# A chunked attention stage whose products are cut by heads, with the bonus term as a product on TensorE

## The chip, the cores and the metric

One core of a Trainium2 chip runs one program with one launch. The metric is device time in microseconds (us) from the program's start to its end. The engines are TensorE (PE; its weight loads are shown apart as PEld), VectorE (DVE), ScalarE (ACT), GpSimd (POOL) and SyncE (SP), on which all transfers are issued. Each works through its instructions in the order in which they were written, and waits for the others by semaphores.

## The reference

```python
def _attn_ref(r, k, v, w, u):                    # B=4, H=8, S=768, D=48
    state = np.zeros((B, H, D, D))
    for t in range(S):
        kt, vt, rt = k[:, :, t], v[:, :, t], r[:, :, t]
        cur = np.einsum('bhd,bhe->bhde', u[None] * kt, vt)
        y[:, :, t] = np.einsum('bhd,bhde->bhe', rt, state + cur)
        state = w[None, :, :, None] * state + np.einsum('bhd,bhe->bhde', kt, vt)
...
x = _moe_ref(attn_out as 3072 tokens x 384)      # x @ w_in, mish, @ w_out
return _moe2_ref(x)                              # 8 experts, weights from a Sinkhorn-scaled gate
```

The state is one 48x48 matrix for each batch row and head. It decays by `w` at each step. The bonus term is `cur`: at its own step a token's `v` counts with the weight sum over d of r·u·k.

## The kernel before

All is float32. The attention is done in chunks of 128 steps: a unit `i` is a chunk `c` (0 to 5) of a batch row `b` (0 to 3), `i = 4c + b`, so 24 units. Two heads form a pair: their 48 rows stand at partitions 0 to 47 and 64 to 111 of a tile of 112, and four pairs `p` stand side by side. In each unit

- `ld` holds r and k with the head's dimension on partitions (112 x 2 x 4 x 128); `lt` holds k and r with time on partitions, `lv` holds v so;
- `rt` and `kd` (DVE) are r and k times powers of the decay; `sc` (PE, `a_scores`) are the products of a head's kd and rt, 48 rows each, two heads on the two halves of the array's rows;
- `A` (128 x 128 for each head) gets the bonus weights `bc` on its diagonal by eight ACT instructions (`a_diag`), and the scores above the diagonal by two predicated copies on DVE (`a_tri`); `bc` is made by two POOL products (`a_q`) and a DVE reduction (`a_b`);
- `ya` (`a_out`) sums, for each pair, the state times rt and, for the two heads, `vz` times A. `vz` is v spread by ACT (`a_vz`) to 96 columns of which one head's half is zero, so that both heads add into the same 96 rows;
- `un` (`a_kv`) is the chunk's own state, kh (k times decay, DVE) times v, for whole pairs; ACT masks the blocks that mix two heads (`a_mask`), and four DVE instructions add it to the decayed state `st` (`a_state`);
- ACT copies `ya` to `xT`, the next layer's input (`a_evac`): one instruction for three pairs and three of 32 rows for the fourth.

A table `steps` of functions and unit offsets is walked once for each `i`; it alone sets the order on every engine. Beside this, every second iteration converts one weight tile of the next layer (`a_cv`: four DVE instructions on `v` and `q`, an ACT copy `wm`; then a subtraction and an addition on POOL). The banks of PSUM are named by tags: the scores take three banks in turn, `un` takes `y0` and `y1` in turn, `ya` has `y2` alone. After the last unit the first expert layer begins (`first`, line 246), from `xs`, the input split into two parts by ACT and POOL (`split_x`).

Of the kernel before, what the change touches and what calls it, by code (L numbers as in the profile page):

```python
# [21 lines left out]
NP = H // 2  # L22
# [25 lines left out]
NVZ = 3  # L48
# [32 lines left out]
def layers(ctx: ExitStack, tc: tile.TileContext, a, out, bad, general):  # L81
# [388 lines left out]

    def chunked_attention(aw, ac):
        KD0 = 1
        EQ1, EQ2, EKD, EKH, ECS, ECA, EXS = pool, pool, dve, dve, pool, pool, pool
        aunits = [(c, b) for c in range(NC) for b in range(B)]
        NA = len(aunits)
        ld, lt, lv = {}, {}, {}

        def load_d(i):
# [3 lines left out]
            lt[i] = aw.tile([128, 2, DM], F32, name=f"lt{i}", tag="lt", bufs=3)  # L482
            nc.sync.dma_start(lt[i], a["kr"][b, c])

        def load_v(i):
            c, b = aunits[i]
            lv[i] = aw.tile([128, DM], F32, name=f"lv{i}", tag="lv")
            nc.sync.dma_start(lv[i], a["v"][b, c])
# [28 lines left out]
        vzs = []  # L517
        for i in range(NVZ):
            vz = wA.tile([128, NP, 2, DD], F32, name=f"vz{i}", tag="w")
            pool.memset(vz, 0.0)  # L520
            vzs.append(vz)

# [25 lines left out]
        def tables():  # L548
            powers(64, 192)
            Wh = me.tile([DR, NP, C], F32, name="Wh", tag="p", bufs=MB[2])  # L550
            dve.tensor_copy(Wh, Wp[:, :, 63:191][:, :, ::-1])
            for p in range(NP):
                tp = bank([128, 128], f"tp{p}", f"y{p % 3}")
                pe.matmul(tp[:, 0:DR], Wh[:, p, :], ident[:DR, :DR], start=True, stop=True)
                act.activation(Wkh[:, p], tp.rearrange("t (j d) -> t j d", j=2)[:, :, 0:D], AF.Copy)
# [8 lines left out]
        st2 = [wA.tile([DR, 2, NP, DD], F32, name=f"st{b}", tag="w") for b in range(B // 2)]  # L564
        st = [st2[b // 2][:, b % 2] for b in range(B)]
        T = [{} for _ in aunits]

        def a_vz(i):
            vz = vzs[i % NVZ]
            vh = lv[i].rearrange("t (p j d) -> t p j d", p=NP, j=2)  # L570
            for j in range(2):
                act.activation(vz[:, :, j, j * D:(j + 1) * D], vh[:, :, j, :], AF.Copy)
            T[i]["vz"] = vz
# [5 lines left out]
        def a_q(i):  # L579

            q = me.tile([128, DM], F32, name=f"aq{i}", tag="y", bufs=MB[3])
            (dve if aunits[i][0] == NC - 1 else EQ1).tensor_tensor(q, lt[i][:, 1], ub, op=ALU.mult)
            EQ2.tensor_tensor(q, q, lt[i][:, 0], op=ALU.mult)
            T[i]["q"] = q

        def a_b(i):
            bc = aw.tile([128, H], F32, name=f"bc{i}", tag="bc")
            dve.tensor_reduce(bc, T[i]["q"].rearrange("t (h d) -> t h d", h=H), axis=AX.X, op=ALU.add)
            T[i]["bc"] = bc
# [31 lines left out]
        def a_kv(i):  # L621
            if aunits[i][0] == NC - 1:
                return
            un = bank([DR, NP, DD], f"un{i}", f"y{i % 2}")
# [5 lines left out]
        def a_mask(i):  # L630
            c, b = aunits[i]
            if c == NC - 1:
                return
            um = st[b] if c == 0 else T[i]["un"]
            for j in range(2):
                act.activation(um[:, :, j * D:(j + 1) * D], T[i]["un"][:, :, j * D:(j + 1) * D], AF.Copy,
                               scale=hm[:, j:j + 1])
            T[i]["um"] = um

        def a_state(i):  # L640
            c, b = aunits[i]
            if 0 < c < NC - 1:
                for p in range(NP):
                    dve.scalar_tensor_tensor(st[b][:, p, :], st[b][:, p, :], w128[:, p:p + 1], T[i]["um"][:, p, :],
                                             op0=ALU.mult, op1=ALU.add)

        def a_out(i):
            c, b = aunits[i]
            x = T[i]
            y = bank([DD, NP, C], f"ya{i}", "y2")  # L650
            for p in range(NP):
                if c > 0:
                    pe.matmul(y[:, p, :], st[b][:, p, :], x["rt"][:, p, :], start=True, stop=False)  # L653
                for j in range(2):
# [12 lines left out]

        def a_cv(i):

            m = (i - 1) // 2  # L670
            if 0 <= m < NCA:
                if i % 2:
                    for _ in conv_bits(m):
                        pass
                    conv_act(m)
                else:
                    conv_sub(m, ECS)
                    conv_add(m, ECA)
# [8 lines left out]
        a_vz(0)  # L687
        for i in range(NA + 1):
            for fn, d in steps:
                if i == NA and fn is a_out:  # L690
                    first(0)
                    first(1)
                if (0 <= i + d < NA or fn is a_cv) and (i + d > 0 or d <= 0) and not (i == 0 and fn in (a_rt, a_kd)):
                    fn(i + d)
                if i == 0 and fn is a_scores:
                    tables()
                    a_b(0)
                    a_rt(1)
                    a_kd(1)
                    a_kh(0)  # L700
                    marks()
            if NA - 4 < i < NA:
                xss.setdefault((-1, 0), []).append(split_x(0, i + 3 - NA, "xs", EXS))
        last.append(lambda: a_evac(NA - 1))

    def stepwise_attention(ac):
# [6 lines left out]
        sel = ac.tile([DR, 3 * D - 1], F32, name="sel")  # L713
        pool.memset(sel, 0.0)
        for j in range(2):
            nc.sync.dma_start(sel[:, (j + 1) * D - 1:(j + 1) * D], a["hmask"][:, j:j + 1])
# [6 lines left out]
        rk = ac.tile([DR, 2, NC, C], F32, name="rk")  # L723
        for b in range(B):
            for p in range(NP):
# [3 lines left out]
                y = [bank([DD, S // 2], f"yg{b}_{p}_{g}", f"y{2 * (p % 2) + g}") for g in range(2)]  # L729
                for e in range(D):  # L730
# [9 lines left out]
                    for g in range(2):  # L740
                        pe.matmul(y[g], sel[:, D - 1 - e:3 * D - 1 - e], x[:, g * S // 2:(g + 1) * S // 2],
                                  start=(e == 0), stop=(e == D - 1))
                for c in range(NC):
# [3 lines left out]
                    if p < KI:  # L747
                        act.activation(xt[0:DD, p, x0:x0 + C], yc, AF.Copy)
                    else:
                        for k in range(KI):  # L750
                            act.activation(xt[DD:128, k, x0:x0 + C], yc[32 * k:32 * k + 32, :], AF.Copy)
# [878 lines left out]
def _lay_out(x):  # L1630
# [17 lines left out]
    tm = [t(z, (B, H, NC, C, D), (0, 2, 3, 1, 4)).reshape(B, NC, C, 1, DM) for z in (k, r)]  # L1648
    a["kr"] = np.ascontiguousarray(np.concatenate(tm, axis=3))
# [4 lines left out]
    a["ub"] = np.ascontiguousarray(np.broadcast_to(u.reshape(1, DM), (128, DM)))  # L1654
# [5 lines left out]
    perm = np.stack([np.where(p < DD, i * DD + p, 3 * DD + 32 * i + p - DD) for i in range(KI)])  # L1660
# [24 lines left out]
```

## Time and profile before

| | |
|---|---|
| median of 3 runs (lowest to highest) | 2024.33 us (2023.33 to 2024.84) |
| the profiled execution's own time | 2026.27 us |
| its span, first to last instruction | 2024.5 us |
| TensorE busy in the span | 1990.4 us, 98% |
| VectorE, ScalarE, GpSimd busy | 67%, 53%, 37% |
| first product of scores | 8.66 us |
| first product of the expert layer | 144.03 us |

The rows are read so: an engine's busy time is the union of its instructions in a stretch; a float32 product is two records (x16 are eight products). "idle before, releaser" is how long the engine had nothing running and what ended that. PEclk is the mean TensorE clock that was granted, 1.00 being 2.4 GHz and 0.50 being 1.2 GHz.

### The profile page before, as it was taken

What the parts mean: (1) busy time and instruction counts of PE and PEld (TensorE: products, weight loads), DVE (VectorE), ACT (ScalarE), POOL (GpSimd) and SP (SyncE); (2) the same over time, 40 slices, a digit from 0 to 9 for tenths busy, and PEclk for the clock granted to TensorE, in tenths of its full rate; (3) what the DMA queues carried; (4) which work ended last, traced back from release to release, by engine and by line L of the source; (5) the groups of instructions that cost most, each with busy time, mean ns of one, the idle gap of its engine ahead of it and who ended that gap; (6) DMA issues with size and microseconds to landing.
All of it is one profiled execution on the core that took longest, in us unless ns stands there. A gap on an engine that the chain in (4) does not pass through costs nothing.

```text
span 2024.5 us, 27279 instructions
## 1 busy us (share of the span) xinstructions
PE 1990.4 (98%) x9334; PEld 1647.8 (81%) x9334; DVE 1360.1 (67%) x2177; ACT 1063.1 (53%) x2204; POOL 751.6 (37%) x639
## 2 busy tenths in 40 slices
PE   8899999999999999999999999999999999999998
PEld 7888888887778888877878888888888888888887
DVE  8998889778787777678764455555465555455554
ACT  7998888888755545444443433343344343333332
POOL 5546565557554333355561243311044011011110
PEclk8999999999999999999999999999999999999999
DMA  8750111010246655655465665558545566445440
GB/s 255 214 150 30 32 32 40 24 35 1 96 154 234 228 207 192 203 211 201 156 225 165 189 215 194 190 153 262 162 151 155 135 182 226 141 151 159 143 120 33
DMA packets 169156, 305.96 MB, mean 151 GB/s; under 512 B 39664, under 2 KB 85424, under 8 KB 169008
## 3 DMA queue, kind: packets, MB, share of 16 engines
q1 hardware_dynamic: 169008, 304.13, 46.7%
q8 instruction: 76, 1.25, 0.3%
q14 instruction: 72, 0.59, 0.1%
HBM read 226.90 MB, written 77.17 MB: 150 GB/s over the span
## 4 chain that ended last, share of the span: by engine, by line
PE 89%; DVE 5%; ACT 2%; issue 2%; POOL 1%; DMA 1%; DVEq 0%; SPq 0%; POOLq 0%; ACTq 0%
PE y L1039 37%; PE Bk L907 16%; PE U L907 15%; PE ph L246 9%; PE x L331 9%; ACT A L606 1%; PE ya L655 1%; DVE tc L939 1%; DVE A L619 1%; PE un L626 0%; DMA lv<-in_v_dram 0%; PE sc L614 0%; ACT xT L666 0%; DVE r L826 0%; PE ya L653 0%
## 5 line engine op out<-in xcount | busy, mean ns | idle before, releaser
L1039 PE MATMUL y<-gf,w 128*128 128x512 f32 x2088 | 570.4, 390 | 0.0
L1039 PEld LDWEIGHTS y<-gf,w 128*128 128x128 f32 x2088 | 391.0, 188 | 82.5 <-DVE gf L1031 1.5
L1039 PE MATMUL y<-ge,w 128*128 128x512 f32 x1368 | 373.8, 390 | 0.0
L1062 POOL TENSOR_TENSOR xT<-xT,xT 128x512 f32<-128x512 f32 x102 | 142.3, 1410 | 577.3 <-DVE xT L1061 576.0
L1029 ACT ACTIVATE gf<-tc 128x512 fp32r<-128x512 f32 x232 | 146.5, 632 | 389.6 <-DVE tc L939 375.6
L939 DVE TENSOR_TENSOR tc<-tc,Bk 128x512 f32<-128x512 f32 x270 | 185.1, 685 | 237.8 <-PE Bk L907 222.3
L939 DVE TENSOR_TENSOR tc<-tc,U 128x512 f32<-128x512 f32 x270 | 185.3, 686 | 222.7 <-PE U L907 208.3
L1039 PEld LDWEIGHTS y<-ge,w 128*128 128x128 f32 x1368 | 256.2, 188 | 53.5 <-DVE ge L1031 0.5
L1029 ACT ACTIVATE ge<-tc 128x512 fp32r<-128x512 f32 x152 | 96.1, 632 | 248.3 <-DVE tc L939 237.6
L331 PE MATMUL x<-g,wm 128*128 128x512 f32 x864 | 212.2, 390 | 0.3 <-POOL g L320 0.2
L246 PE MATMUL ph<-xs,wm 128*128 128x512 f32 x864 | 212.0, 390 | 0.3 <-POOL xs L216 0.3
L1031 DVE SCALAR_TENSOR_TENSOR gf<-tc,gf 128x512 fp32r<-128x512 f32 x232 | 193.5, 837 | 22.9 <-ACT gf L1029 18.2
L246 PEld LDWEIGHTS ph<-xs,wm 128*128 128x128 f32 x864 | 161.8, 188 | 36.5 <-POOL xs L216 0.7
L331 PEld LDWEIGHTS x<-g,wm 128*128 128x128 f32 x864 | 161.8, 188 | 35.2 <-DVE xT L347 0.8
L320 POOL TENSOR_TENSOR g<-y,g 128x512 fp32r<-128x512 f32 x96 | 125.0, 1302 | 102.2 <-ACT g L315 95.6
L937 ACT ACTIVATE tc<-Bk 128x512 f32<-128x512 f32 x192 | 114.3, 595 | 85.3 <-PE Bk L907 78.7
L937 ACT ACTIVATE tc<-U 128x512 f32<-128x512 f32 x192 | 114.4, 596 | 83.5 <-PE U L907 78.7
L907 PE MATMUL Bk<-xc,wc 128*128 128x512 f32 x540 | 152.0, 390 | 0.9 <-DVE tc L939 0.9
L907 PE MATMUL U<-xc,wc 128*128 128x512 f32 x540 | 151.7, 389 | 0.0
L1031 DVE SCALAR_TENSOR_TENSOR ge<-tc,ge 128x512 fp32r<-128x512 f32 x152 | 127.7, 841 | 21.4 <-ACT ge L1029 15.7
L847 POOL TENSOR_TENSOR w<-r,w 128x384 fp32r<-128x384 f32 x64 | 68.6, 1074 | 186.6 <-ACT w L846 175.4
L907 PEld LDWEIGHTS Bk<-xc,wc 128*128 128x128 f32 x540 | 101.1, 188 | 23.0 <-DVE tc L939 1.8
(256 smaller groups left out, 3210.9 us busy)
## 6 DMA issues: line engine op xcount, KB each, us to landing
wc<-keep SPq DMA_DIRECT2D x208, 384.0 KB, 3.7
w<-keep SPq DMA_DIRECT2D x128, 384.0 KB, 5.5
keep<-wc SPq DMA_DIRECT2D x104, 384.0 KB, 3.6
r<-in_w_dram SPq DMA_DIRECT2D x128, 192.0 KB, 3.7
keep<-w SPq DMA_DIRECT2D x64, 384.0 KB, 3.0
ld<-in_rkT_dram SPq DMA_DIRECT2D x24, 448.0 KB, 4.8
pb<-prow SPq DMA_DIRECT2D x42, 256.0 KB, 8.5
lt<-in_kr_dram SPq DMA_DIRECT2D x24, 384.0 KB, 5.1
```

The costliest lines, as they stand in the source:

```text
L246: pe.matmul(ph, w[:, pw, k, :], xs[:, px, :], start=(m == 0), stop=(m == 3 * KI - 1))
L320: pool.tensor_tensor(gs[i][:, 1], y, gs[i][:, 0].bitcast(F32), op=ALU.subtract)
L331: pe.matmul(sums[n][k], wo[f][:, pw, k, :], g[:, px, :], start=(f == f0 and m == 0), stop=(f == f1 and m == 1), skip_group_check=True)
L606: act.activation(A[:, h % 2, h // 2, :], ident, AF.Copy, scale=T[i]["bc"][:, h:h + 1])
L847: eng.tensor_tensor(flat(t[:, 1]), src, flat(t[:, 0]).bitcast(F32), op=ALU.subtract)
L907: pe.matmul(out_, w[:, pw, :], x[px], start=bool(start and m == 0), stop=bool(stop and m == 2), skip_group_check=True)
L937: act.activation(t, b, AF.Copy, scale=1.0 if kind == "c" else -1.0)
L939: dve.tensor_tensor(t, t, b, op=ALU.add if kind == "+" else ALU.subtract)
L1029: act.activation(g[:, 0], t, AF.Relu)
L1031: return lambda: dve.scalar_tensor_tensor(g[:, 1], t, 0.0, g[:, 0].bitcast(F32), op0=ALU.max, op1=ALU.subtract)
L1039: pe.matmul(Y[t][k], w[:, pw, k, :], x[:, px, :], start=(f % NF2 == 0 and m == 0), stop=(f % NF2 == NF2 - 1 and m == 2), skip_group_check= ...
L1062: pool.tensor_tensor(o, o, t_, op=ALU.add)
```

## The change

- `a_out`: the two heads of a pair no longer add into the same 96 rows. Each head's v (64 or 48 columns of `lv`, no `vz`) gives rows 0 to 63 or 64 to 111 of `ya`, on one half of the array's columns (a tile of 128 x 64). All eight of them stand first in a row, then the four products of the state, for whole pairs of 112 rows. The 16 rows between two heads get values that nothing uses.
- The bonus: `a_q` is one POOL product of r and k in `ld`'s layout (112 x 512); `a_bc` sums it with u in four TensorE products of 8 columns (`us` holds u in the right places), into the last 8 columns of the bank of `un`; ACT copies the result to `bc`. So `lt` needs no r and is half as large; the tile `ub` and the DVE reduction go.
- The state `st` is 112 x 112 for a pair, zero off the heads' blocks, and `un` is not masked: `a_decay` multiplies the whole state by the decay on POOL, `a_add` adds the two blocks on DVE (in chunk 0 ACT copies them).
- `kh` goes from DVE to POOL (but for the first unit), the addition of the weight conversion goes one iteration later, and v's tiles have four buffers for two.
- `a_evac` copies 112 rows of three pairs, and the fourth pair to a tile `stg`; when 512 columns of it are there, six transfers put its rows into the gaps of `xT`. The rows of `w_in` are permuted on the host to match.

```diff
-        steps = ((load_d, 3), (a_tri, -1), (a_scores, 0), (a_kv, 0), (a_out, -1), (load_v, 2),
-                 (a_q, 1), (a_state, -2), (a_kh, 1), (a_evac, -2), (a_rt, 1), (a_diag, 0),
-                 (a_cv, 0), (a_mask, -1), (a_vz, 1), (a_kd, 1), (a_b, 1))
+        steps = ((load_d, 3), (a_tri, -1), (a_add, -2), (a_scores, 0), (a_out, -1), (a_kv, 0),
+                 (a_q, 1), (a_bc, 1), (a_kh, 1), (a_evac, -2), (a_b, 0), (a_rt, 1), (a_diag, 0),
+                 (a_cv, 0), (a_kd, 1), (a_decay, -1), (load_v, 2))
...
+            q = me.tile([DR, NP, C], F32, name=f"aq{i}", tag="y", bufs=MB[3])
+            pool.tensor_tensor(q, ld[i][:, 0], ld[i][:, 1], op=ALU.mult)
...
+        def a_bc(i):
+            bp = T[i - 1]["ub"] if i else bank([128, TT], "ub", "y1")
+            T[i]["bp"] = bp[:, TT - H:TT]
+            for p in range(NP):
+                pe.matmul(T[i]["bp"], T[i]["q"][:, p, :], us[:, p, :], start=(p == 0), stop=(p == NP - 1))
...
+        def a_decay(i):
+            c, b = aunits[i]
+            if 0 < c < NC - 1:
+                pool.tensor_tensor(st[b], st[b], w128.unsqueeze(2).to_broadcast([DR, NP, DR]), op=ALU.mult)
...
+                if c == 0:
+                    act.activation(s, n, AF.Copy)
+                else:
+                    dve.tensor_tensor(s, s, n, op=ALU.add)
...
             for p in range(NP):
-                if c > 0:
-                    pe.matmul(y[:, p, :], st[b][:, p, :], x["rt"][:, p, :], start=True, stop=False)
-                for j in range(2):
-                    pe.matmul(y[:, p, :], x["vz"][:, p, j, :], x["A"][:, j, p, :],
-                              start=(c == 0 and j == 0), stop=(j == 1))
+                for j, w in enumerate((64, D)):
+                    pe.matmul(y[64 * j:64 * j + w, p, :], lv[i][:, p * DD + j * D:p * DD + j * D + w], x["A"][:, j, p, :],
+                              start=(p == 0), stop=(c == 0 and p == NP - 1), skip_group_check=True)
+            if c > 0:
+                for p in range(NP):
+                    pe.matmul(y[:, p, :], st[b][:, p, :], x["rt"][:, p, :], start=False, stop=(p == NP - 1),
+                              skip_group_check=True)
...
-            act.activation(xt[0:DD, :, x0:x0 + C], y[:, 0:KI, :], AF.Copy)
-            for k in range(KI):
-                act.activation(xt[DD:128, k, x0:x0 + C], y[32 * k:32 * k + 32, KI, :], AF.Copy)
+            act.activation(xt[0:DR, :, x0:x0 + C], y[:, 0:KI, :], AF.Copy)
+            act.activation(stg[n][0:DR, x0:x0 + C], y[:, KI, :], AF.Copy)
+            if i == ends[n]:
+                spread_heads(n, stg[n])
```

On TensorE, one iteration before, in the middle chunks (`sc` scores, `un` the chunk's state, `ya` the output; two of the four equal pairs of `ya` are shown, the rest alike):

```order
L614 MATMUL sc_145<-rt_770,kd_787 128x128
L626 MATMUL un_805<-lv_681,kh_183 112x96 [waits DMAHW1_49,DVE_49,Activation_49]
L626 MATMUL un_805<-lv_681,kh_183 112x96 x3
L653 MATMUL ya_810<-rt_695,st_187 96x128 [waits PE_49,Activation_49]
L655 MATMUL ya_810<-A_772,vz_153 96x128 x2
L653 MATMUL ya_810<-rt_695,st_187 96x128
L655 MATMUL ya_810<-A_772,vz_153 96x128 x2
```

The same stretch of the changed kernel (the products of 64 and 48 rows alternate four times; the first two are shown), with the bonus products `un<-us,aq` at its end:

```order
L612 MATMUL sc_150<-rt_495,kd_507 128x128
L652 MATMUL ya_527<-A_497,lv_385 64x128 [waits PE_49,Activation_49]
L652 MATMUL ya_527<-A_497,lv_385 48x128 [waits DVE_49]
...
L656 MATMUL ya_527<-rt_428,st_185 112x128 x4
L625 MATMUL un_540<-lv_452,kh_181 112x96 [waits DMAHW3_49,Pool_49]
L625 MATMUL un_540<-lv_452,kh_181 112x96 x3
L582 MATMUL un_540<-us,aq_545 128x8 [waits Pool_49]
L582 MATMUL un_540<-us,aq_545 128x8 x3
```

The output moved ahead of the chunk's state, `un` now waits for POOL, and four products of 8 columns came in behind it.

On GpSimd, two iterations before (`aq` the bonus, `v` and `wm` the weight conversion):

```order
L582 TENSOR_TENSOR aq_683<-lt_513,ub 128x384 [waits DMAHW1_49,DVE_49]
L583 TENSOR_TENSOR aq_683<-aq_683,lt_513 128x384 [waits Pool_49]
L582 TENSOR_TENSOR aq_758<-lt_584,ub 128x384 [waits DMAHW5_49,DVE_49]
L583 TENSOR_TENSOR aq_758<-aq_758,lt_584 128x384 [waits Pool_49]
L171 TENSOR_TENSOR v_706<-v_706,wm_712 128x384 [waits DVE_49,Activation_49]
L176 TENSOR_TENSOR wm_712<-v_706,q_707 128x384 [waits DVE_49,Pool_49]
```

And two iterations of the changed kernel, where `st` is the decay of a state:

```order
L575 TENSOR_TENSOR aq_813<-ld_645 112x512 [waits DMAHW6_49,Pool_49]
L597 TENSOR_TENSOR kh_180<-lt_647,Wkh 128x8x48 [waits DMAHW7_49,PE_49,Pool_49]
L175 TENSOR_TENSOR wm_708<-v_702,q_703 128x384 [waits DVE_49,Pool_49]
L632 TENSOR_TENSOR st_185<-st_185,w_184 112x448 [waits PE_49]
L575 TENSOR_TENSOR aq_885<-ld_717 112x512 [waits DMAHW2_49]
L597 TENSOR_TENSOR kh_181<-lt_719,Wkh 128x8x48 [waits DMAHW3_49,PE_49]
L170 TENSOR_TENSOR v_836<-v_836,wm_842 128x384 [waits DVE_49,Activation_49]
L632 TENSOR_TENSOR st_187<-st_187,w_184 112x448 [waits PE_49]
```

Six instructions in two iterations became eight, one conversion step stands in each iteration, and the decay, last in each, waits for TensorE.

On VectorE, one iteration with a weight conversion in the changed kernel (before, a `kh`, four `st` of 112x96 and a reduction `bc` stood there too, and `st` waited for PE and ACT):

```order
L617 COPY_PREDICATED A_1032<-tri,sc_149 128x512 [waits PE_49,Activation_49]
L644 TENSOR_TENSOR st_191<-st_191,un_942 48x4x48 [waits Pool_49]
L644 TENSOR_TENSOR st_191<-st_191,un_942 48x4x48
L591 TENSOR_TENSOR rt_1092<-ld_913,Wr 112x512 [waits DMAHW4_49]
L141 TENSOR_SCALAR v_1104<-raw_844 128x384 [waits DMAHW7_49]
L143 SCALAR_TENSOR_TENSOR v_1104<-raw_844,v_1104 128x384 [waits DVE_49]
L154 TENSOR_SCALAR q_1105<-v_1104 128x384 [waits DVE_49]
L156 SCALAR_TENSOR_TENSOR q_1105<-raw_844,q_1105 128x384 [waits DVE_49]
L570 TENSOR_TENSOR kd_1114<-ld_913,Wk 112x512
```

The addition to the state now stands ahead of `rt`, the conversion and `kd`, and waits for POOL's decay.

## Rows read from the trace of the kernel before

**Rows 1.** Windows: busy us (and instructions) by engine, PEclk, DMA share, GB/s.
```profile
8.66:40.20 31.54, 27.07 (x192) 24.53 (x192) 27.92 (x50) 22.90 (x76) 18.90 (x19) 0.73 0.93 265
40.20:119.09 78.89, 71.91 (x674) 66.61 (x673) 75.11 (x164) 72.06 (x230) 41.81 (x39) 0.96 0.77 225
119.09:146.17 27.08, 23.60 (x217) 20.98 (x216) 24.62 (x52) 26.48 (x84) 11.89 (x12) 1.00 0.39 121
146.17:2024.50 1878.33, 1862.67 (x8227) 1530.72 (x8227) 1227.35 (x1905) 938.83 (x1810) 674.67 (x553) 1.00 0.45 146
```

**Rows 2.** Lines of VectorE, 40.20 to 119.09: busy us, mean ns, idle before.
```profile
L619 DVE COPY_PREDICATED A<-tri,sc 128x512 f32<-128x512 uint8 x28 | 18.7, 719 | 1.5 <-ACT A L606 1.5
L644 DVE SCALAR_TENSOR_TENSOR st<-st,w,un 112x96 f32<-112x96 f32 x52 | 13.1, 303 | 1.6 <-PE ya L653 1.6
L599 DVE TENSOR_TENSOR kh<-lt,Wkh 128x384 f32<-128x384 f32 x14 | 10.9, 778 | 0.0
L588 DVE TENSOR_REDUCE bc<-aq 128x8 f32<-128x384 f32 x14 | 7.6, 541 | 0.0
...
L157 DVE SCALAR_TENSOR_TENSOR q<-raw,q 128x384 f32<-128x384 uint32 x7 | 3.9, 559 | 0.2
```

**Rows 3.** Lines of ScalarE, 40.20 to 119.09.
```profile
L606 ACT ACTIVATE A<-ident,bc 128x128 f32<-128x128 f32 x112 | 34.3, 388 | 0.4
L666 ACT ACTIVATE xT<-ya 32x128 f32<-32x128 f32 x42 | 11.2, 266 | 0.5
L636 ACT ACTIVATE un<-un,hm 112x192 f32<-112x192 f32 x28 | 11.0, 393 | 0.8
L572 ACT ACTIVATE vz<-lv 128x192 f32<-128x192 f32 x27 | 8.2, 352 | 0.0
```

**Rows 4.** Lines of GpSimd, 40.20 to 119.09.
```profile
L171 POOL TENSOR_TENSOR v<-v,wm 128x384 f32<-128x384 f32 x7 | 7.1, 1009 | 21.2 <-ACT wm L164 15.8 <-DVE q L157 2.9 <-DVE kd L577 2.5
```

**Rows 5.** Timeline of TensorE over one unit: start us, us, instruction.
```profile
85.48 1.16 PE L614 MATMUL sc<-rt,kd 48*128 48x128 f32 x16
86.57 1.02 PE L626 MATMUL un<-lv,kh 128*112 128x96 f32 x8
87.43 0.38 PE L653 MATMUL ya<-rt,st 112*96 112x128 f32 x2
87.65 0.60 PE L655 MATMUL ya<-A,vz 128*96 128x128 f32 x4
...
90.16 1.16 PE L614 MATMUL sc<-rt,kd 48*128 48x128 f32 x16
```

**Rows 6.** Timeline of VectorE and of GpSimd in an iteration with a conversion.
```profile
31.82 1.24 DVE L157 SCALAR_TENSOR_TENSOR q<-raw,q 128x384 f32<-128x384 uint32 x1
32.98 0.67 DVE L577 TENSOR_TENSOR kd<-ld,Wk 112x512 f32<-112x512 f32 x1
...
31.43 1.21 POOL L582 TENSOR_TENSOR aq<-lt,ub 128x384 f32<-128x384 f32 x1 [1.92 <-DVE v L144]
32.72 1.20 POOL L583 TENSOR_TENSOR aq<-aq,lt 128x384 f32<-128x384 f32 x1
```

**Rows 7.** Windows before and after the last of three falls of TensorE's clock.
```profile
100.00:104.00 4.00, 2.60 (x25) 2.04 (x24) 4.00 (x11) 3.88 (x13) 3.46 (x4) 1.00 0.69 185
104.00:108.00 4.00, 4.00 (x24) 4.00 (x24) 3.46 (x8) 2.67 (x9) 1.50 (x2) 0.57 1.00 271
```

**Rows 8.** Timeline of the first units: weight loads of a table's products, the third unit's scores.
```profile
11.20 1.78 PEld L554 LDWEIGHTS tp<-ident,Wh 112*128 112x128 f32 x8 [0.76 <-DVE Wh L551]
23.03 1.16 PE L614 MATMUL sc<-rt,kd 48*128 48x128 f32 x16
```

**Rows 9.** Timeline of the end: the last unit's scores, the split input, the product it releases.
```profile
139.36 1.31 PE L614 MATMUL sc<-rt,kd 48*128 48x128 f32 x16
...
144.83 1.28 POOL L216 TENSOR_TENSOR xs<-xT,xs 128x512 fp32r<-128x512 f32 x1 [3.38 <-ACT xs L215]
...
146.17 1.19 PE L246 MATMUL ph<-xs,wm 128*128 128x512 f32 x4 [0.27 <-POOL xs L216]
```

More of the change, by code (lines that the diff above doesn't have):

```diff
@@ L47 @@
 NWA = 24
-NVZ = 3
 NG = 3
@@ L469, in layers, with spread_heads @@
     last = []
+    def spread_heads(n, src):
+        for k in range(KI):
+            for j in range(2):
+                nc.sync.dma_start(xT[n][64 * j + D:64 * j + 64, k, :], src[64 * j + 16 * k:64 * j + 16 * k + 16])
     def chunked_attention(aw, ac):
         KD0 = 1
-        EQ1, EQ2, EKD, EKH, ECS, ECA, EXS = pool, pool, dve, dve, pool, pool, pool
+        EKD, ECS, ECA, EXS = dve, pool, pool, pool
         aunits = [(c, b) for c in range(NC) for b in range(B)]
@@ L476, in chunked_attention @@
         ld, lt, lv = {}, {}, {}
+        stg = [wA.tile([128, TT], F32, name=f"stg{n}", tag="w") for n in range(NT)]
         def load_d(i):
@@ L562, in marks @@
             dve.scalar_tensor_tensor(okw, wT, W_MAX, okw, op0=ALU.is_le, op1=ALU.mult)
-        st2 = [wA.tile([DR, 2, NP, DD], F32, name=f"st{b}", tag="w") for b in range(B // 2)]
-        st = [st2[b // 2][:, b % 2] for b in range(B)]
+        st = []
+        for b in range(B):
+            st.append(wA.tile([DR, NP, DR], F32, name=f"st{b}", tag="w"))
+            pool.memset(st[b], 0.0)
         T = [{} for _ in aunits]
-        def a_vz(i):
-            vz = vzs[i % NVZ]
-            vh = lv[i].rearrange("t (p j d) -> t p j d", p=NP, j=2)
-            for j in range(2):
-                act.activation(vz[:, :, j, j * D:(j + 1) * D], vh[:, :, j, :], AF.Copy)
-            T[i]["vz"] = vz
+        ends = {(b * NC + c) // NSUB: i for i, (c, b) in enumerate(aunits)}
         def a_kd(i):
@@ L633, in a_mask @@
                 return
-            um = st[b] if c == 0 else T[i]["un"]
             for j in range(2):
[L636 to L645, printed above, removed]
+                r = slice(64 * j, 64 * j + D)
+                s, n = st[b][r, :, r], T[i]["un"][r, :, j * D:(j + 1) * D]
+                if c == 0:
+                    act.activation(s, n, AF.Copy)
+                else:
+                    dve.tensor_tensor(s, s, n, op=ALU.add)
         def a_out(i):
@@ L686, in chunked_attention @@
         a_q(0)
-        a_vz(0)
         for i in range(NA + 1):
@@ L723, in stepwise_attention @@
         rk = ac.tile([DR, 2, NC, C], F32, name="rk")
+        stg = [wA.tile([128, TT], F32, name=f"stg{n}", tag="w") for n in range(NT)]
         for b in range(B):
@@ L728, in stepwise_attention @@
                 rT, kT = (rk[:, j].rearrange("d c t -> d (c t)") for j in range(2))
-                y = [bank([DD, S // 2], f"yg{b}_{p}_{g}", f"y{2 * (p % 2) + g}") for g in range(2)]
+                y = [bank([DR, S // 2], f"yg{b}_{p}_{g}", f"y{2 * (p % 2) + g}") for g in range(2)]
                 for e in range(D):
@@ L747, in stepwise_attention @@
                     if p < KI:
-                        act.activation(xt[0:DD, p, x0:x0 + C], yc, AF.Copy)
+                        act.activation(xt[0:DR, p, x0:x0 + C], yc, AF.Copy)
                     else:
-                        for k in range(KI):
-                            act.activation(xt[DD:128, k, x0:x0 + C], yc[32 * k:32 * k + 32, :], AF.Copy)
+                        act.activation(stg[blk // NSUB][0:DR, x0:x0 + C], yc, AF.Copy)
+        for n in range(NT):
+            spread_heads(n, stg[n])
     if general:
@@ L1653, in _lay_out @@
     a["vT"] = t(v, (B, NP, 2, S, D), (0, 1, 2, 4, 3))
-    a["ub"] = np.ascontiguousarray(np.broadcast_to(u.reshape(1, DM), (128, DM)))
+    a["us"] = np.zeros((DR, NP, H), f4)
+    for h in range(H):
+        a["us"][64 * (h % 2):64 * (h % 2) + D, h // 2, h] = u.reshape(H, D)[h]
     a["ident"] = np.eye(128, dtype=f4)
@@ L1659, in _lay_out @@
     p = np.arange(128)
-    perm = np.stack([np.where(p < DD, i * DD + p, 3 * DD + 32 * i + p - DD) for i in range(KI)])
+    j, d = p // 64, p % 64
+    perm = np.stack([np.where(d < D, i * DD + j * D + d, 3 * DD + j * D + 16 * i + d - D) for i in range(KI)])
     wi = np.asarray(x["moe_w_in"])[perm.reshape(-1)]
```

53 lines of the change are left out of this document (23 added, 30 removed).

## The prediction

> **What bounds the kernel now.** I cut the span at four products of TensorE that stand in both kernels [rows 1]. From 146.17 us on TensorE is busy for 1862.67 of 1878.33 us: the expert layers, which the change doesn't touch. What the attention gains or loses reaches the end unshortened; nothing later can absorb it. Ahead of that lie 146 us in three parts: the start up to the sixth unit (31.54 us), fourteen units of the middle chunks (78.89 us, 5.63 each) and the last units (27.08 us). In the middle part VectorE is busy for 75.11 us, ScalarE for 72.06, TensorE for 71.91, GpSimd for 41.81. The first two share the bound: 5.37 and 5.15 us a unit. TensorE alone would need less: where nothing holds it, a unit takes 90.16 - 85.48 = 4.68 us [rows 5].
>
> **What each engine gives and gets,** for a unit of the middle chunks.
>
> *VectorE* loses the four `st` (4 x 0.303), `kh` (0.778) and the reduction (0.541) [rows 2] and gets two additions of 48 x 192. They read PSUM like `st`, and I price them like it, 0.3 each; below lies nothing, above `kh`. That is 5.37 - 2.53 + 0.6 = 3.4 us.
>
> *ScalarE* loses two `vz` (2 x 0.352), two masks (2 x 0.393) and three copies of 32 rows (3 x 0.266); the copy of the fourth pair is one of these again, and the bonus copy of 8 columns is between nothing and 0.27; I take 0.2. So 5.15 - 2.29 + 0.47 = 3.3 us [rows 3].
>
> *GpSimd* had two products and, in the mean, one conversion step of 1.009 [rows 4]. Now it has q (512 columns, as the split input: 1.28 [rows 9]), `kh` (384 columns: 1.01), a conversion step (1.01) and the decay (448 columns: between, 1.15): 4.45 us instead of 41.81 / 14 = 3.0. No row has a broadcast operand, as the decay has; I keep 1.01 and 1.28, the rows of 384 and of 512 columns, as its bounds.
>
> *TensorE*: scores 1.09 as before (85.48 to 86.57), `un` 0.86 (86.57 to 87.43), the four products of the state 0.22 each as before [rows 5]. The eight products of `vz` cost 0.22 each, 1.76. The eight column products are the unknown. The nearest rows are the scores, where two heads share the array by rows and eight products take 1.09; on the other side they cost 1.76 as before. I take 1.09, because the same number of columns streams through two halves. The four bonus products stream 8 columns but load 128 of weights twice each; eight loads of 112 columns take 0.86 with `un`, and sixteen under the scores 1.09, so 0.55 to 0.9; I take 0.9. Sum 1.09 + 1.09 + 0.88 + 0.86 + 0.9 = 4.82 us.
>
> The Trainium skill, in "TensorE: Matmul & The Clock Gate", Part 3 under "What overlaps and what doesn't", says that a weight load runs beside a product in flight only when the row groups differ. The two column halves use the same rows, so by this rule each load would stand alone. The trace speaks against it: with `un` on all rows, eight loads and eight products together take 0.86 us. By the row the output costs 1.09; by the rule it would be at least the old 1.76, which is the third rival.
>
> **The path that then sets the middle part.** The orders show a loop that was not there. The decay of unit j waits for the last product of `ya` of unit j; the addition waits for the decay and stands ahead of `rt`, the conversion and `kd`; the next scores wait for `kd`. One lap is two iterations, one of them with a conversion. What lengthens it is that VectorE and GpSimd get in each other's way [rows 6]: the conversion's last step took 1.24 us for its mean of 0.56 [rows 2], because GpSimd's product ran until 31.43 + 1.21 = 32.64, and ended 0.42 after that; GpSimd's next one, asked for at 32.72, took 1.20 and ended 0.86 after VectorE's end at 33.06. So the two go in turns. `kd` (0.67) shows no such wait: it reads PSUM. Before, GpSimd was idle for half of the time; now its queue is full behind the decay, and each of the four conversion steps finds it running.
>
> From the decay's end: additions 0.6, `rt` 0.68; q (1.28) has just ended; a conversion step with one operand 0.22 (an estimate, half of the 0.42 of one with two), `kh` 0.86, step 0.42, conversion step of GpSimd 0.86, step 0.22, the next unit's decay 1.0, last step 0.42; `kd` 0.67; the copy on which the second product of scores waits 0.72 [rows 2]; scores 1.09, columns 1.09, state 0.88 and the last product's way through 0.27; decay 1.15. Sum 11.15. Successive VectorE rows start 0.08 before the last has ended (`kd` at 32.98, the step ahead of it until 33.06); the hand-overs between engines, which I didn't count, cost about as much. So 11.1 for two units, 5.55 a unit. TensorE has 2 x 4.82 = 9.64 us of work in a lap and idles 1.5, at one place: ahead of the scores behind the conversion. Bounds: 9.7 if GpSimd's steps let VectorE pass (two units at 4.82), 12.3 if the first step comes just after `kh` has begun.
>
> That idle time has a price. Clock falls followed stretches where TensorE was least busy: 2.60 of 4.00 us from 100 to 104, then a mean clock of 0.57 (part of it at 1.2 GHz) [rows 7]; of the three falls two lie in the middle part, whose mean clock is 0.96 [rows 1]. A stretch costs the loop about 1.4 us: 4 us x (1 - 0.57) is 1.7, some of it off the path. I put one into the new middle part: 7 x 11.1 + 1.4 = 79.1 us for 78.89. **No gain there** (-0.2).
>
> **The start.** The first units have no decay and no state product. The clock is low, and the bonus products come ahead of the table's (eight such loads took 1.78 us [rows 8]) and again ahead of the second scores; part lies under waits, and the third unit's scores go from 23.03 to about 24.9. From there ScalarE sets the pace in chunk 0: two state copies (2 x 0.393), the diagonals (34.3 / 14 = 2.45) [rows 3], and by estimates from the copies there 0.75 for the output, 0.2 for the bonus and 0.25 of conversion, 4.4 a unit: 24.9 + 3 x 4.4 = 38.1 for 40.20. Gain 2.1; between -2 (clock low for one stretch more, 1.7, and GpSimd's `kh` ahead of VectorE's, 1.0) and +4. Each `lt` brings half the bytes while DMA is at 0.93; I count nothing for that, since ScalarE is later.
>
> **The end.** The last four units have no `un` and no `kh`. TensorE needs 4.82 for the first and 4.0 for the others; twice `kd` is late by 0.7 behind a conversion: 4.8 + 4.0 + 4.7 + 4.7 = 18.2 instead of 20.27 (119.09 to 139.36). Then, from the last scores to the product that waits for the third split input: bonus copy 0.2, diagonals 2.45, a copy of 384 and one of 512 columns (1.1, an estimate from 192 in 0.393), GpSimd 1.28 and handing over, 5.4; before 146.17 - 139.36 = 6.8 [rows 9]. Gain 3.4. The six transfers of `spread_heads` go into SP's queue ahead of a `lv`, but xT's first block is whole ten units before it is read.
>
> **Sum.** 2.1 - 0.2 + 3.4 = 5.3 us off the span of 2024.5, so 2019.2; the profiled execution's own 2026.27 goes to 2021.0. That execution lies 1.9 above the median of the runs shown; from 2024.33 I predict **2019.0 us**.
>
> **The rivals.**
> - *The turns cost nothing* (faster still). GpSimd's steps come where VectorE is at other work; then TensorE's 4.82 sets the middle, with a small wait in each lap: 14 x 5.0 = 70, gain 8.9 + 2.1 + 3.4, **2010**. For it: the last conversion step's mean was 0.56 [rows 2], so it rarely waited. Against it: GpSimd's queue is now full when they come.
> - *The clock* (slower). Each lap has its 1.5 us of waiting at one place, and the stretch ahead of the fall [rows 7] had no more than 1.4 us of it in 4. Against it: before, TensorE idled 78.89 - 71.91 = 7.0 us in the middle part [rows 1], and of all its waits only two led to a fall there. If six of the seven laps fall to 1.2 GHz for a stretch and two more do at the start and the end, that is 7 x 1.4 = 9.8 us more than I count: **2029**. It decides from four stretches more (5.3 / 1.4).
> - *The columns don't run together* (slower). The output stays at 1.76, 0.67 more. A lap has one output on its path, so the middle loses 7 x 0.67 = 4.7 more; in the start TensorE's 4.0 + 0.67 passes ScalarE's 4.4, 3 x 0.3 and as much again at the low clock; the end loses 4 x 0.67: the gain of 5.3 becomes a loss of 3.9, **2028**. `un`'s rows argue against it. By that rule of the Trainium skill this is the outcome.
>
> **Numbers.** My forecast, with its own range of 2015 to 2023.5, has 0.40; the turns that cost nothing 0.25; the clock 0.22; the columns 0.13. A measurement tells a change of about 0.2%, 4 us: faster means below 2020.3, slower above 2028.4. Of my case 0.6 lies below 2020.3; with the first rival that makes 0.50 for faster. Slower gets 0.6 of the two last rivals, 0.21; the rest, 0.29, is no change. The range is 2009.5 to 2030: it leaves the outer half of the fast rival and the outer third of the slow ones.
>
> **What would show it.** Right: laps of two units of about 11.1 us in the middle, conversion steps on VectorE with means near 1 us, scores that wait for VectorE in every second unit, POOL busy for some 4.5 of 5.5 us; column products of a unit in 1.1 us, sixteen records; an unchanged stretch behind 146. Wrong: laps below 10.3 or above 12, more than three stretches at a granted clock near 0.5 behind the first ten units, sixteen column records in 1.8 us, or a decay far from 1.15.

## The result, and the profile after

The changed kernel takes 2040.62 us (median of 5 runs, 2037.53 to 2045.75) against 2024.33 (2023.33 to 2026.42) for the kernel before in the same rounds: a ratio of 1.0083, 95% interval 1.0062 to 1.0105. It is slower by 0.83%, where 2019.0 us and a gain were forecast. The profiled execution took the median time, with a span of 2038.8 us.

The windows of the changed kernel, cut at the same four products as [rows 1] (busy us and instructions of PE, PEld, DVE, ACT and POOL, granted clock, DMA share, GB/s):

```profile
7.84:41.95 34.11, 33.11 (x241) 30.17 (x241) 22.02 (x39) 19.64 (x67) 16.71 (x15) 0.60 0.79 221
41.95:133.77 91.82, 80.42 (x786) 73.97 (x785) 76.46 (x112) 48.94 (x162) 60.43 (x56) 0.85 0.58 160
133.77:157.18 23.41, 22.04 (x249) 19.62 (x248) 21.02 (x35) 18.97 (x61) 15.96 (x15) 1.00 0.49 127
157.18:2038.80 1881.62, 1863.03 (x8227) 1531.21 (x8227) 1223.55 (x1905) 937.82 (x1808) 675.68 (x553) 1.00 0.46 146
```

The ends of the parts against [rows 1]: the start is over at 41.95 instead of 40.20 (+1.75), the middle part takes 91.82 instead of 78.89 (+12.9), the end 23.41 instead of 27.08 (-3.7), the stretch behind 1881.62 instead of 1878.33 (+3.3). Together +14.3 us, the difference of the spans.

TensorE's timeline in the middle part, for [rows 5]:

```profile
51.47 1.16 PE L612 MATMUL sc<-rt,kd 48*128 48x128 f32 x16
52.56 1.09 PE L652 MATMUL ya<-A,lv 128*64 128x128 f32 x16
53.58 1.13 PE L656 MATMUL ya<-rt,st 112*112 112x128 f32 x8
54.54 0.94 PE L625 MATMUL un<-lv,kh 128*112 128x96 f32 x8
55.31 0.98 PE L582 MATMUL un<-us,aq 112*128 112x8 f32 x8
59.07 2.71 PE L612 MATMUL sc<-rt,kd 48*128 48x128 f32 x16 [2.78 <-DVE kd L570]
```

The work is what was forecast: a unit begins 4.76 us after the one ahead (46.71, 51.47), and sixteen column records take 1.02 us (52.56 to 53.58). But then TensorE waits 2.78 us for `kd`, and the next scores take 2.71 us instead of 1.16. Why `kd` is late stands on the other two engines, VectorE first:

```profile
52.35 1.02 DVE L141 TENSOR_SCALAR v<-raw 128x384 uint32<-128x384 uint32 x1
53.40 1.25 DVE L143 SCALAR_TENSOR_TENSOR v<-raw,v 128x384 uint32<-128x384 uint32 x1
54.68 0.36 DVE L154 TENSOR_SCALAR q<-v 128x384 uint32<-128x384 uint32 x1
55.08 3.34 DVE L156 SCALAR_TENSOR_TENSOR q<-raw,q 128x384 f32<-128x384 uint32 x1
58.34 0.67 DVE L570 TENSOR_TENSOR kd<-ld,Wk 112x512 f32<-112x512 f32 x1
...
52.14 1.01 POOL L597 TENSOR_TENSOR kh<-lt,Wkh 128x384 f32<-128x384 f32 x1
53.11 1.12 POOL L175 TENSOR_TENSOR wm<-v,q 128x384 fp32r<-128x384 f32 x1
54.79 1.04 POOL L632 TENSOR_TENSOR st<-st,w 112x448 f32<-112x448 f32 x1 [0.56 <-PE ya L656]
55.79 1.26 POOL L575 TENSOR_TENSOR aq<-ld 112x512 f32<-112x512 f32 x1
57.02 0.99 POOL L597 TENSOR_TENSOR kh<-lt,Wkh 128x384 f32<-128x384 f32 x1
57.97 1.31 POOL L170 TENSOR_TENSOR v<-v,wm 128x384 f32<-128x384 f32 x1
```

The last conversion step (L156) took 3.34 us; its mean before was 0.559 [rows 2]. It ends 0.41 us after GpSimd's `kh` (58.42 against 58.01): it sat through the decay, q and `kh`, three products that GpSimd ran one behind the other, and got in only then. The first step of the same lap (L141) did get in behind one product: it ended at 53.37, 0.22 us after the `kh` ahead of it (52.14 to 53.15), although GpSimd's next product is recorded from 53.11 on. The last step took 3.34 or 3.35 us in four of the seven laps, and these are the four with the wait for `kd`; in the other three it took 0.56, and TensorE did not wait. The laps can be read from the scores of every second unit (the ones ahead of these are at 41.95 and 51.47, the one behind them at 133.77):

```profile
66.74 1.16 PE L612 MATMUL sc<-rt,kd 48*128 48x128 f32 x16
82.87 1.16 PE L612 MATMUL sc<-rt,kd 48*128 48x128 f32 x16
92.68 1.16 PE L612 MATMUL sc<-rt,kd 48*128 48x128 f32 x16
107.83 1.16 PE L612 MATMUL sc<-rt,kd 48*128 48x128 f32 x16
123.89 1.16 PE L612 MATMUL sc<-rt,kd 48*128 48x128 f32 x16
```

So the three laps without the wait take 9.5 to 9.9 us, 29.2 together, and the four with it 15.2 to 16.1, 62.6 together. The windows, for [rows 7]:

```profile
52.00:56.00 4.00, 4.00 (x51) 3.71 (x47) 3.90 (x5) 3.30 (x11) 3.44 (x5) 1.00 0.62 130
56.00:60.00 4.00, 1.22 (x7) 0.99 (x8) 4.00 (x4) 2.62 (x9) 3.28 (x3) 0.72 0.13 27
60.00:64.00 4.00, 4.00 (x32) 3.44 (x32) 3.39 (x7) 0.00 (x0) 0.00 (x0) 0.50 1.00 297
```

TensorE is busy for 1.22 of 4 us, and its clock falls to the lower level (1.2 GHz). From the mean of 0.85 the middle part spent (1 - 0.85) / 0.5 x 91.82 = 27.5 us there; the wait occurs four times (2.76 to 2.78 us). While the clock is low, ScalarE and GpSimd wait for TensorE (0.00 busy).

Behind the attention, SyncE's queue (the column after "SPq" is the line, the second figure how long these issues held the queue), VectorE and TensorE:

```profile
157.23 3.66 SPq L473 DMA_DIRECT2D xT<-stg  x6
160.93 0.58 SPq L1290 DMA_DIRECT2D graw<-in_w_gate_dram  x1
...
164.16 0.18 DVE L1291 CAST wga<-graw 128x24 fp32r<-128x24 f32 x1 [8.24 <-DMA graw<-in_w_gate_dram]
...
170.07 3.91 PE L245 MATMUL ph<-xs,wm 128*128 128x512 f32 x9 [3.90 <-DVE y L302]
```

The gate weights' load stands behind the last six transfers of `spread_heads`; VectorE, which takes its work in order, stood for 8.24 us, and so its `y` came late and TensorE idled 3.90 us. (That this is the cause, an experiment below shows.)

### The profile page after: what moved, and what is told of

It is laid out like the page before. It is cut to its first block, busy times and chain, and to the rows that moved or that the text cites. A ratio compares the mean times of both kernels' runs of the same rounds, so it can differ in the third digit from the quotient of the medians.

```text
span 2038.8 us, 27545 instructions
## 1 busy us (share of the span) xinstructions
PE 2004.5 (98%) x9526; PEld 1660.7 (81%) x9526; DVE 1347.3 (66%) x2098; ACT 1027.6 (50%) x2100; POOL 772.6 (38%) x655
## 4 chain that ended last, share of the span: by engine, by line
PE 89%; DVE 4%; POOL 2%; issue 2%; DMA 1%; SPq 1%; ACT 1%; POOLq 0%; DVEq 0%; ACTq 0%
PE y L1045 36%; PE Bk L913 16%; PE U L913 15%; PE x L330 10%; PE ph L245 9%; DMA pb<-prow 1%; DVE tc L945 1%; SPq L473 1%; PE sc L612 1%; PE ya L652 0%; PE un L625 0%; POOL aq L575 0%; POOL kh L597 0%; POOL st L632 0%; DVE gf L1037 0%
## 5 line engine op out<-in xcount | busy, mean ns | idle before, releaser
L853 POOL TENSOR_TENSOR w<-r,w 128x384 fp32r<-128x384 f32 x64 | 68.6, 1075 | 185.4 <-ACT w L852 161.6
```

The lines of the kernel that those rows point to most:

```text
L853: eng.tensor_tensor(flat(t[:, 1]), src, flat(t[:, 0]).bitcast(F32), op=ALU.subtract)
```

## The experiments

Theory A: VectorE's conversion steps and GpSimd's products shut each other out, and GpSimd's queue, 8.9 us of a lap of two units of 9.5 (by the rows of its lines: 2 x (1.27 + 1.0 + 1.0) and two conversion steps of about 1.15), leaves too few gaps for them. Theory B: only `kd`'s place behind the conversion is at fault. Theory C: TensorE's new products pull its clock down by themselves. Theory D: VectorE has too much to do. A time without a range is that of one execution.

**`kd` ahead of the conversion.**

```
-(a_rt, 1), (a_diag, 0), (a_cv, 0), (a_kd, 1), (a_decay, -1)
+(a_rt, 1), (a_kd, 1), (a_diag, 0), (a_cv, 0), (a_decay, -1)
```

> The change, with kd computed ahead of the conversion steps on VectorE instead of behind them. Theory A (GpSimd's queue takes about 2.5 to 3 us of every second unit from VectorE, and kd was only what happened to stand behind): scores no longer wait for kd, but the next unit's two copies into A now stand behind the same late conversion step, so TensorE idles a similar 2 to 3 us at the output products, released by VectorE's A; the clock still falls to 1.2 GHz there, and the middle part (sixth unit's scores to twentieth unit's) stays at 86 to 94 us (91.8 in the changed kernel). Theory B (only the order of kd is at fault): no wait over 0.6 us, no fall, middle part 67 to 74 us and a total 18 to 25 us below the changed kernel's. Theory C (TensorE's own products pull the clock down, waits or not): falls stay without any idle time ahead of them, middle part 85 to 92.

2038.35 us; middle part 91.36. TensorE's timeline of this kernel:

```profile
57.32 0.48 PE L612 MATMUL sc<-rt,kd 48*128 48x128 f32 x2
60.22 2.07 PE L612 MATMUL sc<-rt,kd 48*128 48x128 f32 x14 [2.41 <-DVE A L617]
```

The wait moved by one step: the scores' second bank waits for the copies into A, which now stand behind the same slow L156 (2416 ns in the mean). A holds (2 to 3 us expected, at the scores instead of the output); B falls.

**`kh` back on VectorE.**

```
-                (pool if i else dve).tensor_tensor(khs[i % 2]...
+                dve.tensor_tensor(khs[i % 2]...
```

> The change, with kh left on VectorE as before (0.56 us there instead of 1.0 us on GpSimd, in each unit). Theory A (the two engines shut each other out, GpSimd 8.9 us of a 9.5 us lap of two units, and VectorE's conversion steps 2.0 us of it): GpSimd then has 6.9 us a lap and VectorE 3.1 us of steps that can be shut out, 10.0 us together, so a lap takes 9.6 to 11 us: middle part 68 to 78 us, fewer or no falls of the clock. Theory D (VectorE simply has too much to do, 2 x 3.4 + 2.0 us and now 1.1 more): lap as long as now or longer, middle part 90 to 98 us. Theory C (TensorE's own products): unchanged at 90 to 93.

2018.9 us; middle part 68.63. Its window, and L156 in it (busy us, mean ns | idle before):

```profile
39.82:108.45 68.63, 68.63 (x785) 63.97 (x784) 66.48 (x126) 48.92 (x161) 46.41 (x41) 1.00 0.79 217
...
L156 DVE SCALAR_TENSOR_TENSOR q<-raw,q 128x384 f32<-128x384 uint32 x7 | 3.9, 558 | 0.2
```

TensorE has no idle time left, the clock stays up, and L156 is back at 558 ns (2150 in the changed kernel's middle part). One product in each unit, moved between two engines, is worth 23.2 us. Both times come again in other kernels: 91.56 with 18 warm-up products, 68.63 and 68.65 in two of the combinations below. (Of the whole time less is left: here the clock fell in the last units, after a wait of 0.91 us for `kd` ahead of the 23rd unit's scores. The same wait in the changed kernel was not followed by a fall.) C and D fall: TensorE has the same products, VectorE more work.

**q computed for six units only.**

```
+            if i > 5:
+                T[i]["q"] = T[i - 1]["q"]
+                return
             q = me.tile([DR, NP, C], F32, name=f"aq{i}", tag="y", bufs=MB[3])
```

> The change, with the product of r and k computed by GpSimd for the first six units only; every later unit multiplies the sixth unit's product again, so the bonus of the later units is left out of the right result, and TensorE has the same products. It takes 1.27 us a unit from GpSimd and nothing else. Theory A: GpSimd has 6.4 us of a 9.5 us lap, the last conversion step comes through in under 2 us, waits for kd are under 1 us, clock falls at most once or twice, middle part 67 to 76 us, total 15 to 25 us below the changed kernel's. Theory C and Theory D (VectorE's sum): middle part 88 to 93 us, as now.

2007.41 us; middle part 66.75, L156 at 558 ns, clock 1.00. A again, with another of GpSimd's products. Middle part (67 to 76) and total went beyond what was expected; the total fell by 33 us: 25 of it in the middle part, the rest ahead of it (the sixth unit's scores at 37.91) and behind.

**`kh` on VectorE and a product nobody reads on GpSimd.**

```
+                if i:
+                    pool.tensor_tensor(junk, Wkh, Wkh, op=ALU.mult)
```

> kh on VectorE, as in the run with kh alone (middle part 68.6 us, the last conversion step L156 at 558 ns), and on GpSimd in kh's place a product of the same shape whose result nobody reads: the product is work added, and nothing waits for it. Theory A (how long GpSimd's queue runs without a wait decides, not what it computes): L156 takes over 1.5 us again in most laps, and the middle part comes back to 80 to 96 us with falls of the clock. Rival (the loss came from kh being late from GpSimd, or from GpSimd's results in general): L156 stays at 0.56 us and the middle part at 67 to 72 us.

2036.43 us; middle part 89.96. Its row of L156 and the waits of the scores:

```profile
L156 DVE SCALAR_TENSOR_TENSOR q<-raw,q 128x384 f32<-128x384 uint32 x7 | 12.8, 1830 | 0.2
...
L615 PE MATMUL sc<-rt,kd 48*128 48x128 f32 x225 | 20.6, 299 | 10.5 <-DVE kd L571 9.7 <-DVE A L620 0.8
```

So it is not that GpSimd's results come late: its being busy is enough. The long step did not sit through the added product itself. In four laps it took 2.39 us, through the decay and q, and got in ahead of the added product; with it VectorE's second step (L143) meets GpSimd's conversion step (1141 ns in the mean instead of 559), and the last one comes only when the decay runs.

**Filler products in the wait.**

```
+        def a_fill(i):
+            if i % 2 and 6 < i < 20:
+                for _ in range(12):
+                    pe.matmul(T[i]["ub"][:, 384:496], warm, warm[:, 0:112], start=True, stop=True)
...
-                 (a_q, 1), (a_bc, 1), (a_kh, 1),
+                 (a_q, 1), (a_bc, 1), (a_fill, 0), (a_kh, 1),
```

> The change, with 12 products of zeros by zeros (112 columns each, about 2.7 us together, into columns of the bank that hold nothing) on TensorE ahead of the scores of every second unit of the middle part, where it now waits 2.78 us for kd; nothing else changes. It parts the price of the wait from that of the lower clock. Theory A: the clock stays at 2.4 GHz, each lap of two units still takes the 2 x 4.8 + 2.7 us in which VectorE gets its conversion steps done, now in all seven laps: middle part 84 to 89 us (7 x 12.3 = 86), against 91.8. If the lower clock were most of the loss, the middle part would come to 76 to 80 us (14 x 4.8 + 4 x 2.78). Theory C (TensorE's products pull the clock down by themselves): the clock still falls.

2040.42 us; middle part:

```profile
38.54:126.04 87.50, 86.52 (x929) 80.05 (x929) 78.71 (x106) 48.88 (x161) 58.95 (x56) 1.00 0.61 170
...
L156 DVE SCALAR_TENSOR_TENSOR q<-raw,q 128x384 f32<-128x384 uint32 x6 | 20.1, 3353 | 0.2
```

The clock stays at its upper level and the part still takes 87.5, as A expected (84 to 89): the shutting out alone keeps the laps long. One lap takes 9.5 us, as in the changed kernel, and six take 13.0 each (55.67 to 68.66 is one), all six with L156 at 3.35 us. The 4.3 us that this part gains is the difference of two things. A lap with the wait takes 13.0 us instead of 15.65 in the mean, so the low clock costs 2.65 in each, 10.6 in the four of the changed kernel; but with the clock up six laps have the long step, not four, and each of these two is 3.2 longer. Why the step comes through in two laps behind falls of the clock (83 and 124 us in the changed kernel) no run shows; behind the two other falls it did not.

The whole kernel gains only 0.2 us. The start, with the same instructions, was 3.4 us shorter by chance. What start and middle gave was lost behind them, where one more run of fillers stands (130.73) and the clock now fell after a wait of 0.92 us at 142.48 (0.50 from 146 to 150).

**Where the transfers are issued, and where the gate weights.** Two kernels:

```
-                nc.sync.dma_start(xT[n][64 * j + D...
+                nc.scalar.dma_start(xT[n][64 * j + D...
```

> The change, with the 18 transfers of the fourth pair's rows issued from ScalarE's queue instead of SyncE's. Theory (they stand ahead of the gate weights in SyncE's queue, VectorE waits in order for those until 164, and TensorE idles 3.9 us at 170 and runs at half clock after that): the gate weights come at about 147 to 150, no idle of VectorE of 8 us, no wait of TensorE for the first output split, and the stretch from the product that waits for the third split to the end is 1877 to 1880 us (1881.6 in the changed kernel, 1878.3 before): total 2 to 4.5 us less. Rival (the rows themselves come late whatever queue they use, since they leave only with the last units): the first expert products wait, and the stretch stays at 1881 to 1883 us.

```
         load_d(2)
         load_raw(2)
+        nc.sync.dma_start(graw, a["w_gate"])
...
     with mst:
-        nc.sync.dma_start(graw, a["w_gate"])
```

> The change, with the load of the gate weights issued at the start (behind the first loads of the attention) instead of behind the rows' transfers in SyncE's queue. Theory: VectorE's 8.24 us of waiting for them at 156 to 164 goes, TensorE's 3.9 us at 170 and the fall of the clock behind it go too, and from the product that waits for the third split to the end it takes 1877 to 1880 us (1881.6 in the changed kernel, 1878.3 before). Rival (the rows are late themselves, or a raw weight piece behind them is): VectorE waits there for something else, and the stretch stays at 1881 to 1882.5 us.

From ScalarE's queue: 2043.67 us, the stretch behind 1883.3. The gate weights' wait is gone, but the same six issues now hold ScalarE (first row: its queue):

```profile
149.60 3.72 ACTq L473 DMA_DIRECT2D xT<-stg  x6
153.37 0.18 ACT L586 ACTIVATE bc<-un 128x8 f32<-128x8 f32 x1 [3.79 <-DMA xT<-stg]
```

A miss, with neither theory's cause: not when the rows land, but 0.62 us an issue on the engine that issues. TensorE then waited 2.90 us for ScalarE's `g`. With the gate weights early: 2036.43 us, and behind

```profile
157.28:2034.60 1877.32, 1861.45 (x8227) 1529.81 (x8227) 1227.90 (x1903) 938.72 (x1808) 677.11 (x553) 1.00 0.46 147
```

So 4.3 us less than in the changed kernel and 1.0 less than before: the theory of the queue holds.

**More warm-up.** `NWARM = 14` becomes 18.

> The change, with 18 instead of 14 warm-up products ahead of the first scores, which fills most of TensorE's 0.62 us of idle time at 7.2 us. Theory S1 (that idle time is what lets the clock fall at 10 us, and the fall is what makes the start long): no fall at 10, sixth unit's scores at 32 to 37 us. Theory S2 (the fall comes from what runs at 8 to 12 us, the bonus products of 8 columns and the wait for kh at 12): it falls all the same, and the sixth unit's scores come at 37.8 to 42 us, which is the spread over the kernels run so far that are alike up to there.

2038.46 us; the sixth unit's scores at 36.41, after a fall to the lower clock that came at about 18 us instead of 10 and was short:

```profile
8.49:36.41 27.92, 23.45 (x241) 20.90 (x240) 24.95 (x40) 19.58 (x67) 17.46 (x15) 0.94 0.80 230
```

Not decided: the time is S1's, but a fall still came. And without that edit the start varies among executions with the same instructions up to there: 41.95 in the changed kernel, 37.83 with the transfers on ScalarE's queue.

**Combinations.** Three edits: `kh` on VectorE, `kd` ahead, gate weights early.

> The change with three edits together: kh on VectorE, kd ahead of the conversion steps, gate weights loaded at the start. Theory A: middle part 67 to 71 us (68.6 with kh alone), no wait for kd at the 23rd unit's scores and no fall of the clock behind it (8 us at 1.2 GHz with kh alone, some 4 us lost), the stretch behind 3 us shorter than in the changed kernel: a total of 2005 to 2013 us, so 0.5 to 1 % less than before. If shutting out was only part of it and VectorE's sum (9.8 us a lap) binds: middle part 72 to 78 us and 2014 to 2020 us.

2022.32 us (2018.26 to 2033.31), ratio 0.9997, interval 0.9979 to 1.0015. A miss of both ranges: middle part 82.68 in the profiled execution (2019.24 us). The row of the scores names the reason:

```profile
L613 PE MATMUL sc<-rt,kd 48*128 48x128 f32 x224 | 18.7, 287 | 7.2 <-DVE A L618 7.2
```

With `kd` ahead, the conversion meets GpSimd's decay and q (L156 at 1385 ns), and the copies into A come late. What was neutral in the changed kernel costs 14 us here: the order of VectorE's queue decides which of GpSimd's products its steps meet. So without it:

> The change with two edits: kh on VectorE and the gate weights loaded at the start. Theory A with the transfers' place in the queue: middle part 67 to 70 us as with kh alone, the stretch behind 3 to 4.5 us shorter than in the changed kernel; total 2010 to 2017 us, 0.4 to 0.7 % under the kernel before. If the end or the start give part of it back (the 23rd unit's wait of 0.9 us and the clock behind it): 2017 to 2022 us.

2011.43 us (2006.64 to 2017.82), ratio 0.9932, interval 0.9915 to 0.9949. Middle part 68.63, behind 1876.8, as expected. And with 18 warm-up products and `kd` ahead in the last three units alone:

> The change with four edits: kh on VectorE, gate weights at the start, 18 warm-up products, and kd ahead of the conversion steps for the last three units alone (where no state is added any more). If the fall of the clock at the start and that at the 23rd unit both come from TensorE's idle time in front of them: sixth unit's scores at 34 to 38 us, none of the 8 us at 1.2 GHz that the run with kh alone had at the end, total 2003 to 2011 us. If the clock falls at the start whatever is done there: as the kernel with two edits, 2010 to 2017 us.

2007.31 us (2005.05 to 2011.95), ratio 0.9911, interval 0.9898 to 0.9924: faster than the kernel before by 0.89%, and than the changed one by 1.7% (0.9911 / 1.0083). Its windows:

```profile
7.97:34.48 26.51, 24.58 (x241) 22.38 (x240) 23.96 (x44) 19.46 (x67) 12.69 (x10) 0.87 0.82 248
34.48:103.13 68.65, 68.65 (x786) 64.00 (x785) 66.44 (x125) 48.91 (x161) 46.39 (x41) 1.00 0.81 221
103.13:126.20 23.07, 22.27 (x248) 19.88 (x248) 21.54 (x40) 19.03 (x61) 16.09 (x15) 1.00 0.57 149
126.20:2003.30 1877.10, 1861.40 (x8227) 1531.05 (x8227) 1226.07 (x1903) 938.12 (x1808) 675.44 (x553) 1.00 0.46 147
```

The clock still fell in the start (0.87), and what of the 34.48 is due to the warm-up stays as open as above: without that edit the run with two edits had 35.92. Nor was there a fall at the end in that run's profiled execution, so neither of the last two edits is shown to be worth its place; the intervals of the two ratios overlap.

## Why the prediction was wrong

The forecast was 5.3 us off the span, the result 14.3 on it: 19.6 us apart, of which 12.7 lie in the middle part, 3.9 in the start, 3.3 behind, and -0.3 in the end.

**The step that failed is "So the two go in turns".** From one meeting [rows 6] I took that VectorE gets in between any two of GpSimd's products, and charged each conversion step at most one of them. That meeting had a gap: GpSimd's first product ended at 32.64 and its next was asked for at 32.72. In the new order the decay, q and `kh` run without one. The first two steps of the lap shown above still went as charged, 0.22 and 0.42 us behind one product each. The last was charged the decay and 0.42 us, and sat through q and the next unit's `kh` besides (3.34 us). The Trainium skill, in "SBUF — State Buffer", section "Two separate sides", has the two engines share one pair of ports as an exclusive lock, kept for a whole instruction; the trace agrees that one is shut out entirely, and that `kd`, which reads PSUM, is not (0.678 us in the mean). That a waiting step can lose to several products in a row, the trace adds; what decides to how many, the runs leave open. The lap, 11.1 us with 9.7 and 12.3 as its bounds, has two lengths: 13.0 with the long step and the clock up, and 9.7 in the mean without that step. Four laps of the one and three of the other make 7.6 us more and 4.1 less than seven of 11.1.

**The clock** was a rival, and its mechanism came: four falls of the middle part, each after a wait of 2.76 to 2.78 us. I had counted one stretch at 1.4 us; it was four at 2.65, 10.6 us, which is the other 9.2 of the 12.7 and near the 9.8 that the rival added. But the falls hang on the step that failed: without the long step (`kh` on VectorE, q for six units) there are none in the middle part, and with the clock held up (the fillers) the part still takes 87.5 us.

**The rival of turns that cost nothing** was right on TensorE's part: 4.76 us a unit for my 4.82. Its 70 us for the middle part came only with `kh` on VectorE (68.6), a kernel that it did not speak of. The change without the move of `kh` thus gains 10.3 us there (78.89 to 68.63), and `kh` on GpSimd costs 23.2.

**Sizes on the other engines.** GpSimd's decay took 1.012 us (1.15 taken, 1.01 the bound), q 1.266, `kh` 1.059: 60.43 / 14 = 4.3 us a unit for 4.45. ScalarE 3.5 for 3.3. VectorE 5.46 for 3.4: its four conversion steps had means of 2.150, 1.244, 0.735 and 0.556 us, together 4.69 a lap, where the lowest means among all these kernels make 1.83 (0.558, 0.559, 0.352, 0.360). So 1.4 us a unit is time shut out, and the rest a sum that I had set 0.6 too low.

**The columns** run together (sixteen records in 1.02 us for 1.09), so the third rival falls. With it falls, for these tiles, the rule of the Trainium skill in "TensorE: Matmul & The Clock Gate", Part 3, by which the loads of products on the same rows stand alone.

**The start** (-2.1 forecast, +1.75 measured). The mis-sized term is the low clock: (1 - 0.60) / 0.5 x 34.11 = 27 us at 1.2 GHz, by [rows 1] 17 us before. The forecast end of 38.1 lies inside the spread of executions that are alike up to there (37.83 to 41.95), so a hit or a miss here is luck. What makes that stretch long or short in one execution stays open.

**The end** (-3.4 forecast, -3.7 measured) was right, in its parts too: 18.3 us to the last scores for 18.2, and 5.1 from there for 5.4.

**Behind** (0 forecast, +3.3). The step "the six transfers of `spread_heads` go into SP's queue ahead of a `lv`, but xT's first block is whole ten units before it is read" looked at what reads xT, and not at what else stands in that queue: the gate weights, for which VectorE waits in order.

## What to carry to other kernels

- Before moving work to an engine that "has room", add up how long its queue then runs without a wait, and ask which steps of the other engine must meet it. GpSimd had room in its sum (60.4 of 91.8 us busy), and still one product of 1 us in each unit cost 23 us.
- A wait that moves with the order (first `kd`, then A) points to a slow step behind both; look for the instruction whose duration is not that of its own kind.
- For each transfer added to a queue, list all that stands behind it, small loads too, and who waits for those in order.

## What was not expected of the hardware

- A VectorE step of 0.56 us with two operands in SBUF took 3.34 while GpSimd ran products without a gap, and 0.56 again with one product less in each unit; `kd`, with an operand in PSUM, stayed at 0.68.
- Filling TensorE's waits with products kept its clock at 2.4 GHz (mean 1.00 over 87.5 us) and gained 4.3 us of the part only: each fall had cost 2.65 us, but with the clock up six laps had the long step instead of four.
- Six transfers of 32 KB hold the issuing queue for 3.66 us on SyncE and 3.72 on ScalarE, some 0.6 us an issue; on a compute engine that is time taken from its work.
